# K and V in 4 MB loads over four slots instead of 2 MB loads over eight, with PV of the second half moved behind all its scores

## The chip, the core, the metric

One core of one Trainium2 chip runs one program. The metric is device time in microseconds (us). A ratio is the mean time of one kernel's runs over the mean time of the other's runs of the same rounds, so it is not quite the ratio of the medians that are quoted beside it.

## The reference, cut to what matters

The program is one decode step of a transformer block: two sequences, one new token each, and a cache of 32,768 keys and values for each of 4 key/value heads. Each key/value head serves 8 query heads. A small modulation and query projection come first; an output projection and a two-layer MLP come last.

```python
B, Sq, D = (2, 1, 1024)
Hq, Hkv, Sk, Dh = (32, 4, 32768, 128)
...
scores = jnp.einsum('bhqd,bhkd->bhqk', q, k) * Dh ** (-0.5)
p = _softmax(scores, axis=-1)
o = jnp.einsum('bhqk,bhkd->bhqd', p, v)
```

K and V together are 2 x 2 x 4 x 32,768 x 128 bf16 values, 134 MB. All the weights are another 44 MB. Every byte is used once. So the question for this kernel is how well its loads keep the DMA engines busy.

## The kernel before

There are 8 rounds, one for each pair of sequence and key/value head. In a round, K comes in 4 chunks of 8,192 rows. PE transposes a chunk in 8 groups, VectorE and ScalarE copy the result out of PSUM, and PE multiplies it with the 8 queries. Softmax and PV (probabilities times V) of a round run one round later, between the chunks of the next K. One chunk of K or V is one load of 2 MB, and each kind and chunk has its own 16 KB slot (per partition).

```python
SLOT = {("K", 0): 0, ("K", 1): 1, ("V", 0): 2, ("V", 1): 3, ("K", 2): 4, ("V", 2): 5, ("K", 3): 6, ("V", 3): 7}
...
add((kind, i, cc), [TPC, D], cache[b, g][r0:r0 + CH_ROWS, :].rearrange("(p t) d -> p t d", p=128),
    SLOT[kind, cc] * 16 * KB, f"{kind}{cc}")
...
order = [("K", 0), ("K", 1), ("V", 0), ("V", 1), ("K", 2), ("V", 2), ("K", 3), ("V", 3)]
early = [("V", 0), ("V", 1), ("K", 0), ("K", 1), ("K", 2), ("V", 2), ("K", 3), ("V", 3)]
```

All loads form one list. SyncE issues them strictly in that order. Before each issue it waits until the last reader of the slot's old content is done. So one load that must wait for its slot holds back everything behind it.

```python
for cc in range(NCH):
    for g8 in range(TPC // 8):
        tr(i, cc, g8)                 # transposes: the last reader of a K slot
        ...
    if cc == 1:
        lagged(lambda: pv(i - 1, 0), row_sums, lambda: pv(i - 1, 1))
    elif cc > 1:
        lagged(lambda: pv(i - 1, cc)) # the last reader of a V slot
```

## Time and profile before

| | before |
|---|---|
| median of 3 runs | 423.7 us (423.6 to 423.91) |
| span of the profiled run | 421.8 us |
| bytes moved, mean rate | 178.47 MB, 423 GB/s |
| share of the load queue's packets in 16 engines' span | 99.1% |
| PE, VectorE, ScalarE busy | 71%, 40%, 37% |
| last landing to the end of the span | 415.98 to 421.8 us |

These lines are from the page of the kernel before. The rows PEclk, DMA and GB/s are the span in 40 equal slices: granted PE clock and busy share of the DMA engines in tenths, and the rate. The group line ends with PE's idle time just before such instructions and what ended it. The last two lines give count, size and median time from issue to landing of the loads.

```profile
span 421.8 us, 11638 instructions
...
PEclk9999999969989999796988997898899696655565
DMA  8999999999999999999999999999999999999995
GB/s 334 429 431 423 435 432 423 429 432 426 433 432 429 435 429 430 435 429 429 435 429 432 437 423 433 435 426 433 433 428 433 430 430 435 427 429 424 428 423 244
DMA packets 14335, 178.47 MB, mean 423 GB/s; under 512 B 1513, under 2 KB 1520, under 8 KB 2802
q1 hardware_dynamic: 14322, 178.29, 99.1%
...
DMA 80%; PE 16%; ACT 2%; SPq 1%; issue 0%; DVE 0%
...
L542 PE MATMUL psKT<-ident,K 128*128 128x128 bf16 x2048 | 173.8, 237 | 39.0 <-DMA K<-in_A_k_cache_dram 37.8
...
K<-in_A_k_cache_dram SPq DMA_DIRECT2D x32, 2048.0 KB, 31.6
V<-in_A_v_cache_dram SPq DMA_DIRECT2D x32, 2048.0 KB, 35.1
```

No slice between the first and the last is under 423 GB/s, and PE is the one that waits. The Trainium skill ("DMA: Bandwidth & Descriptors", section Where 436 GB/s comes from) puts the ceiling of a core's 16 DMA engines at 435 GB/s. This trace agrees: 431 GB/s over 120 to 340 us. Only two things can shorten this kernel: a cheaper stream of bytes, or a shorter start or end.

Tools are used below, all of them made from the trace's records of single DMA packets and of the issues.

- *Packet time*: how long the record of a packet lasts. In the load queue a 4-byte packet, which each engine writes at the end of a load, takes 9 ns; 8,192 B take 309.5 ns; 16,384 B take 611 ns.
- *Outstanding*: the bytes of all loads issued before a moment, less the bytes of the packets finished by then.
- *Loss* of a stretch: its length less its bytes at 430 GB/s.

Here is what the packet records say of the kernel before (counted over the load queue; size in bytes, number, ns of one; 305 packets of other sizes are left out):

```
      4   1473     9.0
   7168   1024   272.0
   8192   1792   309.5
  12288   1024   469.3
  16384   8704   611.5
```

The 8,704 packets of 16,384 B are the K and V loads (64 x 128) and the wo loads (4 x 128). So "16 KB per packet" is not new in the change: a partition's 64 rows of a chunk lie together in memory, and the kernel before already moved them as one packet.

### The profile page before, as it was taken

The numbers are of one execution on the slowest core, as the hardware profiler recorded it, in microseconds if no ns is written. First come the engines' busy times: TensorE is split into PE (matmuls) and PEld (weight loads), VectorE is DVE, ScalarE is ACT, GpSimd is POOL, SyncE is SP. The second block draws the span as 40 slices with busy tenths as digits, with TensorE's granted clock in tenths as the row PEclk, the third lists the DMA queues.
The fourth block names the chain that finished last, engine by engine and source line by source line (L and its number), as shares of the span: only waits on it lengthen the run. The fifth ranks groups of instructions, "written<-read, shape, count | busy, mean of one in ns | idle before, by whom it ended". The sixth has DMA issues, their size and how long they took to land.

```text
span 421.8 us, 11638 instructions
## 1 busy us (share of the span) xinstructions
PE 299.5 (71%) x5171; PEld 238.1 (56%) x5171; DVE 167.1 (40%) x347; ACT 156.6 (37%) x269; POOL 6.0 (1%) x31
## 2 busy tenths in 40 slices
PE   1547478878997688587877848796888682445576
PEld 1105158866975678476767828684776671112244
DVE  1102026644663476155534724652474352101311
ACT  2000025547645349142833633383447245000020
POOL 3000000000000000000000000000000000000000
PEclk9999999969989999796988997898899696655565
DMA  8999999999999999999999999999999999999995
GB/s 334 429 431 423 435 432 423 429 432 426 433 432 429 435 429 430 435 429 429 435 429 432 437 423 433 435 426 433 433 428 433 430 430 435 427 429 424 428 423 244
DMA packets 14335, 178.47 MB, mean 423 GB/s; under 512 B 1513, under 2 KB 1520, under 8 KB 2802
## 3 DMA queue, kind: packets, MB, share of 16 engines
q1 hardware_dynamic: 14322, 178.29, 99.1%
q8 instruction: 9, 0.15, 0.1%
q14 instruction: 4, 0.03, 0.0%
HBM read 178.28 MB, written 0.00 MB: 423 GB/s over the span
## 4 chain that ended last, share of the span: by engine, by line
DMA 80%; PE 16%; ACT 2%; SPq 1%; issue 0%; DVE 0%
DMA K<-in_A_k_cache_dram 60%; PE psKT L542 11%; DMA wo<-in_A_wo_dram 8%; DMA w<-in_B_w_dram 7%; DMA wmod<-in_w_mod_dram 4%; PE psS L554 3%; ACT E_sb L575 1%; PE psO L584 1%; SPq L415 1%; ACT KT_sb L546 1%; PE psO L757 1%; PE psS L678 0%; ACT L575 0%; PE psM L565 0%; ACT S_sb L558 0%
## 5 line engine op out<-in xcount | busy, mean ns | idle before, releaser
L542 PE MATMUL psKT<-ident,K 128*128 128x128 bf16 x2048 | 173.8, 237 | 39.0 <-DMA K<-in_A_k_cache_dram 37.8
L542 PEld LDWEIGHTS psKT<-ident,K 128*128 128x128 bf16 x2048 | 133.2, 106 | 49.7 <-DMA K<-in_A_k_cache_dram 44.9
L548 DVE COPY KT_sb<-psKT 128x1024 bf16<-128x1024 bf16 x160 | 108.3, 689 | 112.5 <-PE psKT L542 112.5
L546 ACT ACTIVATE KT_sb<-psKT 128x1024 bf16<-128x1024 bf16 x96 | 98.0, 1020 | 131.2 <-PE psKT L542 131.2
L554 PE MATMUL psS<-qcur,KT_sb 128*128 128x8 bf16 x2048 | 88.2, 167 | 8.1 <-ACT KT_sb L546 6.7
L554 PEld LDWEIGHTS psS<-qcur,KT_sb 128*128 128x128 bf16 x2048 | 79.5, 99 | 13.2 <-ACT KT_sb L546 8.1
L584 PE MATMUL psO<-V,E_sb 128*32 128x512 bf16 x512 | 35.5, 403 | 6.3 <-DMA V<-in_A_v_cache_dram 5.0
L575 ACT ACTIVATE E_sb<-S_sb,negm 128x256 bf16<-128x256 f32 x64 | 32.3, 504 | 7.7 <-DVE negm L571 6.8
L559 DVE TENSOR_REDUCE m1c<-psS 128x8 f32<-128x512 f32 x32 | 22.1, 691 | 14.4 <-ACT S_sb L558 13.3
L558 ACT ACTIVATE S_sb<-psS 128x512 f32<-128x512 f32 x32 | 19.0, 592 | 14.1 <-PE psS L554 14.1
L584 PEld LDWEIGHTS psO<-V,E_sb 128*32 128x32 bf16 x512 | 11.5, 100 | 16.8 <-DMA V<-in_A_v_cache_dram 5.7
L491 PE MATMUL psS<-wmod,inT 128*32 128x512 bf16 x64 | 8.4, 622 | 11.9 <-DMA wmod<-in_w_mod_dram 11.9
L678 PE MATMUL psS<-wo,atT 128*32 128x512 bf16 x64 | 7.6, 627 | 11.3 <-DMA wo<-in_A_wo_dram 11.3
L462 ACT ACTIVATE stat<-stat 128x2 f32<-128x2 f32 x3 | 0.6, 204 | 38.9 <-DVE stat L461 38.9
L512 PE MATMUL psS<-wq,inT 128*32 128x512 bf16 x64 | 7.6, 627 | 6.9 <-DMA wq<-in_A_wq_dram 5.9
L575 ACT ACTIVATION_READ_ACCUMULATOR E_sb<-S_sb,negm 128x1 f32 x64 | 12.1, 189 | 0.0
L491 PEld LDWEIGHTS psS<-wmod,inT 128*32 128x32 bf16 x64 | 1.3, 112 | 17.9 <-DMA wmod<-in_w_mod_dram 17.4
L678 PEld LDWEIGHTS psS<-wo,atT 128*32 128x32 bf16 x64 | 1.9, 128 | 16.3 <-DMA wo<-in_A_wo_dram 10.3
L604 PE MATMUL psM<-msum,hmat 128*128 128x128 f32 x16 | 4.4, 359 | 7.1 <-DVE msum L599 7.1
L497 ACT ACTIVATE S_sb<-psS 128x512 f32<-128x512 f32 x1 | 0.6, 597 | 22.8 <-DVE S_sb L499 22.8
L499 DVE COPY S_sb<-psS 128x512 f32<-128x512 f32 x1 | 0.7, 692 | 20.6 <-PE psS L491 20.6
L599 DVE SCALAR_TENSOR_TENSOR msum<-psO,mk,msum 128x128 f32<-128x128 f32 x24 | 8.4, 351 | 0.8
(116 smaller groups left out, 132.3 us busy)
## 6 DMA issues: line engine op xcount, KB each, us to landing
K<-in_A_k_cache_dram SPq DMA_DIRECT2D x32, 2048.0 KB, 31.6
V<-in_A_v_cache_dram SPq DMA_DIRECT2D x32, 2048.0 KB, 35.1
wmod<-in_w_mod_dram SPq DMA_DIRECT2D x8, 1536.0 KB, 16.5
wq<-in_A_wq_dram SPq DMA_DIRECT2D x4, 2048.0 KB, 37.5
wo<-in_A_wo_dram SPq DMA_DIRECT2D x4, 2048.0 KB, 29.0
w<-in_B_w_dram SPq DMA_DIRECT2D x4, 1792.0 KB, 39.1
w<-in_B_w_dram SPq DMA_DIRECT2D x3, 2048.0 KB, 30.6
w<-in_B_w_dram SPq DMA_DIRECT2D x1, 768.0 KB, 28.0
```

Of the source, the lines that this page charges most:

```text
L491: pe(lambda e, w=it.view, k=k, ch=ch, n=n, q=q: e.matmul(bank[n][32 * q:32 * q + 32, :], lhsT=inT[:, k, :], rhs=w[:, ch * 512:(ch + 1) * 512],
L512: pe(lambda e, w=it.view, k=k, ch=ch, n=n, q=q: e.matmul(bank[n][32 * q:32 * q + 32, :], lhsT=inT[:, k, :], rhs=w[:, k % 2, ch * 512:(ch + ...
L542: pe(lambda e, kq=kq, jj=jj, w=it.view, t=t: e.transpose(psKT[kq][:, jj * 128:(jj + 1) * 128], w[:, t, :], ident[:, :]), reads=[it.reg, "i ...
L546: act(lambda e, src=src: e.activation(KT_sb[g8][:, :, :], src, ACT.Copy), reads=[f"psKT{kq}"], writes=[f"KT_sb{g8}"], sem=f"ev{cc}_{g8}")
L548: dve(lambda e, src=src: e.tensor_copy(KT_sb[g8][:, :, :], src), reads=[f"psKT{kq}"], writes=[f"KT_sb{g8}"], sem=f"ev{cc}_{g8}")
L554: pe(lambda e, t=t, jj=jj: e.matmul(ps[:, t * HPG:(t + 1) * HPG], lhsT=KT_sb[g8][:, jj, :], rhs=qcur[:, :], start=True, stop=True), reads= ...
L558: act(lambda e: e.activation(Sc, ps[:, :].rearrange("p (t h) -> p h t", h=HPG), ACT.Copy), reads=[preg], writes=[f"S_sb{i % 2}_{cc}"], sem ...
L559: dve(lambda e: e.tensor_reduce(m1c[:, :, cc], ps[:, :].rearrange("p (t h) -> p h t", h=HPG), AX.X, ALU.max), reads=[preg], writes=[f"m1c{ ...
L575: act(lambda e: e.activation(E_sb[:, :, h, :], S_sb[j][:, h, :].rearrange("p (u t) -> p u t", t=4), ACT.Exp, bias=negm[:, h:h + 1], scale= ...
L584: pe(lambda e, t4=t4, tg=tg, q=q: e.matmul(psO[32 * q:32 * q + 32, :], lhsT=E_sb[:, tg // 4, :, :].rearrange("p h t -> p (h t)"), rhs=it.v ...
L599: dve(lambda e, q=q: e.scalar_tensor_tensor(out=msum[:, :], in0=psO[:, q * 128:(q + 1) * 128], scalar=mk4[:, q:q + 1], in1=msum[:, :], op0 ...
L678: pe(lambda e, w=it.view, g=g, j=j, hf=hf, q=q: e.matmul(psS[0][32 * q:32 * q + 32, :], lhsT=atT[g][:, j, :], rhs=w[:, j, hf * 512:(hf + 1 ...
```

## The change

Two chunks become one load of 4 MB, which takes one of four 32 KB slots. A slot now comes free only when both of its chunks have been read. PV of chunk 2 moves behind the scores of chunk 3, so that PE does not wait for the second V load in the middle of the second half of K. The number of issues halves and the bytes stay.

```diff
-    SLOT = {("K", 0): 0, ("K", 1): 1, ("V", 0): 2, ("V", 1): 3, ("K", 2): 4, ("V", 2): 5, ("K", 3): 6, ("V", 3): 7}
+    SLOT = {("K", 0): 0, ("V", 0): 1, ("K", 1): 2, ("V", 1): 3}
...
-        add((kind, i, cc), [TPC, D], cache[b, g][r0:r0 + CH_ROWS, :].rearrange("(p t) d -> p t d", p=128),
-            SLOT[kind, cc] * 16 * KB, f"{kind}{cc}")
+        add((kind, i, hf), [2, TPC * D], cache[b, g][r0:r0 + 2 * CH_ROWS, :].rearrange("(c p t) d -> p c (t d)", c=2, p=128),
+            SLOT[kind, hf] * 32 * KB, f"{kind}{hf}")
...
-    order = [("K", 0), ("K", 1), ("V", 0), ("V", 1), ("K", 2), ("V", 2), ("K", 3), ("V", 3)]
-    early = [("V", 0), ("V", 1), ("K", 0), ("K", 1), ("K", 2), ("V", 2), ("K", 3), ("V", 3)]
+    order = [("K", 0), ("V", 0), ("K", 1), ("V", 1)]
+    early = [("V", 0), ("K", 0), ("K", 1), ("V", 1)]
...
-            elif cc > 1:
-                lagged(lambda: pv(i - 1, cc))
+            elif cc == 3:
+                lagged(lambda: pv(i - 1, 2), lambda: pv(i - 1, 3))
```

What is cut: the same split of an index into half and chunk in the transposes and in PV, and new offsets for one w1 load and one w2 load.

More of the change, by code (lines that the diff above doesn't have):

```diff
@@ L368, in add, with add_kv @@
         by_key[key] = it
-    SLOT = {("K", 0): 0, ("K", 1): 1, ("V", 0): 2, ("V", 1): 3, ("K", 2): 4, ("V", 2): 5, ("K", 3): 6, ("V", 3): 7}
-    def add_kv(kind, i, cc):
+    SLOT = {("K", 0): 0, ("V", 0): 1, ("K", 1): 2, ("V", 1): 3}
+    def add_kv(kind, i, hf):
         cache = A_k_cache if kind == "K" else A_v_cache
         b, g = i % 2, i // 2
-        r0 = cc * CH_ROWS
-        add((kind, i, cc), [TPC, D], cache[b, g][r0:r0 + CH_ROWS, :].rearrange("(p t) d -> p t d", p=128),
-            SLOT[kind, cc] * 16 * KB, f"{kind}{cc}")
+        r0 = hf * 2 * CH_ROWS
+        add((kind, i, hf), [2, TPC * D], cache[b, g][r0:r0 + 2 * CH_ROWS, :].rearrange("(c p t) d -> p c (t d)", c=2, p=128),
+            SLOT[kind, hf] * 32 * KB, f"{kind}{hf}")
     wm_v = w_mod.rearrange("(p k) n -> p k n", k=KT8)
@@ L383, in bass_adaLN_cond__gqa_block_cached__mixer_channel_mlp__decode_kernel @@
         add(("wq", k), [2, HQ * D], A_wq[k * 256:(k + 1) * 256, :].rearrange("(k p) n -> p k n", p=128), (96 + 16 * k) * KB)
-    for cc in range(4):
-        add_kv("K", 0, cc)
-    order = [("K", 0), ("K", 1), ("V", 0), ("V", 1), ("K", 2), ("V", 2), ("K", 3), ("V", 3)]
-    early = [("V", 0), ("V", 1), ("K", 0), ("K", 1), ("K", 2), ("V", 2), ("K", 3), ("V", 3)]
+    add_kv("K", 0, 0)
+    add_kv("K", 0, 1)
+    order = [("K", 0), ("V", 0), ("K", 1), ("V", 1)]
+    early = [("V", 0), ("K", 0), ("K", 1), ("V", 1)]
     for i in range(1, NBG + 1):
-        for kind, cc in early if i == 1 else order:
+        for kind, hf in early if i == 1 else order:
             if kind == "V":
-                add_kv("V", i - 1, cc)
+                add_kv("V", i - 1, hf)
             elif i < NBG:
-                add_kv("K", i, cc)
+                add_kv("K", i, hf)
     for g, off in enumerate((128, 144, 0, 16)):
         add(("wo", g), [8, DM], A_wo[g * 1024:(g + 1) * 1024, :].rearrange("(p j) n -> p j n", j=8), off * KB)
-    for k, off in enumerate((64, 96, 32, 48)):
+    for k, off in enumerate((64, 80, 32, 48)):
         add(("w1", k), [2, F], B_w1[k * 256:(k + 1) * 256, :].rearrange("(k p) n -> p k n", p=128), off * KB)
     w2_v = B_w2.rearrange("(q p j) n -> p q (j n)", p=128, j=4)
-    for k, off in enumerate((80, 112, 128)):
+    for k, off in enumerate((96, 112, 128)):
         add(("w2", k), [2, 4 * DM], w2_v[:, 2 * k:2 * k + 2, :], off * KB)
@@ L537, in tr @@
     def tr(i, cc, g8):
-        it = need("K", i, cc)
+        it = need("K", i, cc // 2)
+        kt = it.view[:, cc % 2, :].rearrange("p (t d) -> p t d", d=D)
         kq = g8 % NPKT
@@ L541, in tr @@
             t = g8 * 8 + jj
-            pe(lambda e, kq=kq, jj=jj, w=it.view, t=t: e.transpose(psKT[kq][:, jj * 128:(jj + 1) * 128], w[:, t, :], ident[:, :]),
+            pe(lambda e, kq=kq, jj=jj, w=kt, t=t: e.transpose(psKT[kq][:, jj * 128:(jj + 1) * 128], w[:, t, :], ident[:, :]),
                reads=[it.reg, "ident"], writes=[f"psKT{kq}"], mark=(jj == 7))
@@ L579, in pv @@
     def pv(i, cc):
-        it = need("V", i, cc)
+        it = need("V", i, cc // 2)
+        vt = it.view[:, cc % 2, :]
         for t4 in range(TPC // 4):
@@ L584, in pv @@
             pe(lambda e, t4=t4, tg=tg, q=q: e.matmul(psO[32 * q:32 * q + 32, :], lhsT=E_sb[:, tg // 4, :, :].rearrange("p h t -> p (h t)"),
-                                                    rhs=it.view[:, t4 * 4:t4 * 4 + 4, :].rearrange("p t d -> p (t d)"),
+                                                    rhs=vt[:, t4 * 512:(t4 + 1) * 512],
                                                     start=(cc == 0 and t4 < 4), stop=(cc == NCH - 1 and t4 >= TPC // 4 - 4),
```

## The prediction

> **What bounds the kernel now.** The DMA engines, nearly from first byte to last. The page of before: 178.3 MB in 421.8 us, 423 GB/s, the queue's packets taking 99.1% of the 16 engines' span; between the first and last slice 422 to 437 GB/s. The Trainium skill ("DMA: Bandwidth & Descriptors", section Where 436 GB/s comes from) gives a ceiling of 435 GB/s; this trace agrees, with 430 to 433 in the windows of the K/V stage. PE is busy 71%, DVE 40%, ACT 37%; PE waits for K (37.8 us in the groups); the chain of waits gives DMA 80%. Not DMA time: the start (first slice 334 GB/s) and the 5.8 us after the last landing (415.98).
>
> **What the change touches.**
> - Packet size: nothing. The trace's packet records already hold 8,704 packets of 16,384 B (K, V and wo), 611 ns each.
> - Loads: 64 become 32. Each ends with a 4-byte packet per engine of 9 ns; 32 fewer save about 0.3 us (estimate). Setup and landing latency are hidden: at every K/V issue at least 5.2 MB is outstanding (bytes issued less bytes landed). SyncE's 0.33 us per issue is off the path.
> - Slots: same 128 KB, half as many, so one comes free only after two chunks. This is the danger: the queue could run dry. Estimates from before's landing times and PE times (a chunk takes 6.6 us after idling, 5.2 us warm, PV of a chunk 1 us; the first round with exponentials takes 13.8 us for two chunks):
>  - first K reload: slot free near 74, queue fed until 81;
>  - second: near 84.5, fed until 91;
>  - K of the third round: near 105, fed until 110.6;
>  - steady rounds (39 us of DMA, 27 of PE): 15 us left;
>  - last V load, which waits for the deferred PV: near 348.3, fed until 354.
>  The thinnest margin is 5 to 6 us, over 2 MB; before it was about 12 us.[...]
> - PE: bursts and pauses twice as long, so maybe more work at the lower granted clock; PE has a third of its time to spare.
> - Deferred PV: it delays one V slot (counted above). After the last V landing two chunks of PV remain instead of one, 1 us, hidden behind the wo, w1 and w2 loads queued by then.
>
> **Critical path.** Only the 0.3 us of end packets lies on it.
>
> **Predicted time.** 423.4 us (423.7 less 0.3), range 422.4 to 424.9. Faster by over 2%: 1%; within 2%: 96%; slower by over 2%: 3%.
>
> **What would show the steps.** DMA slices 9 throughout with 425 to 435 GB/s; about 13,800 packets (512 fewer); K and V issues 16 each of 4,096 KB, still 20 to 35 us to landing; PE's wait for K about as long in total, in fewer and longer waits; mean granted clock equal or a little lower. If the queue ran dry, a slice between 75 and 115 us, or near 350 us, would fall below 400 GB/s, and the span would grow by that hole.
>
> **What would make it wrong.** (1) A dry spell at a thin margin: a few us. (2) Alternating between two runs 2 MB apart slows the reads: packets would take over 611 ns; the wq loads, two runs 1 MB apart, ran at 427 GB/s, so I doubt it. (3) SyncE stalls while issuing (wq, two packets per partition, blocked it 3 to 7 us when much was outstanding), harmless while the queue is full.

## The result, and the profile after

| | before | after |
|---|---|---|
| median | 423.73 us (423.6 to 423.91, 6 runs) | 423.51 us (423.41 to 424.64, 6 runs) |
| ratio after / before | | 1.0001, interval 0.9988 to 1.0014 |
| span of the profiled run | 421.8 us | 422.8 us (the 424.64 us run) |

The time is the same. But the runs of after are not one heap: four lie at 423.41 to 423.58, just under before, and two at 424.21 and 424.64. The profiled run is the slowest of them. These are the lines of its page that answer to those above.

```profile
span 422.8 us, 11591 instructions
...
PEclk9999757989999698988788896969887888665566
DMA  8999999999999999999999999999999999999995
GB/s 334 430 429 424 437 426 432 427 398 429 432 428 434 429 429 434 429 432 432 429 434 429 432 434 427 436 428 432 434 428 436 428 432 434 428 432 420 428 425 227
DMA packets 13822, 178.46 MB, mean 422 GB/s; under 512 B 1001, under 2 KB 1008, under 8 KB 2290
q1 hardware_dynamic: 13810, 178.28, 99.0%
...
DMA 70%; PE 26%; ACT 2%; SPq 1%; issue 0%; DVE 0%
...
L543 PE MATMUL psKT<-ident,K 128*128 128x128 bf16 x2048 | 178.0, 240 | 43.3 <-DMA K<-in_A_k_cache_dram 41.9
...
K<-in_A_k_cache_dram SPq DMA_DIRECT2D x16, 4096.0 KB, 25.8
V<-in_A_v_cache_dram SPq DMA_DIRECT2D x16, 4096.0 KB, 32.6
```

Almost every line says what it said before. There are 512 packets under 512 B fewer, which is 32 loads x 16 engines. PE waits for K about as long in total. One thing stands out: the ninth slice (84.6 to 95.1 us) moved 398 GB/s. It also shows what does not mean much here. The chain gives DMA 70% instead of 80%, though the kernel is as DMA-bound as before, because the chain only changes over to PE where a reload waited for PE to free its slot.

The same place, from the windows of the same run (columns: stretch, its us, busy us of each engine with instruction counts, granted clock, DMA share, GB/s) and from the timeline of SyncE:

```profile
85.00:90.00 5.00, 4.03 (x102) 3.82 (x99) 3.27 (x5) 3.09 (x4) 0.00 (x0) 1.00 1.03 436
90.00:95.00 5.00, 3.21 (x48) 2.50 (x45) 2.07 (x5) 1.62 (x2) 0.19 (x1) 0.79 0.96 367
```

```profile
88.51 0.37 SPq L415 DMA_DIRECT2D K<-in_A_k_cache_dram  x1
```

That issue is the second K reload of the kernel (round 1, second half). It had to wait until PE had transposed chunk 3 of round 0. When it went out, 1.15 MB was outstanding, 2.7 us of work at 430 GB/s. The packet records show what followed: between 85 and 97 us, 38 of the 294 packets of 16,384 B took over 640 ns, up to 1,411 ns, and from 90 to 94 us the stream moved 317, 317, 388 and 393 GB/s, us by us. In these 4 us the rate was 18% under 430 GB/s, but the DMA engines' busy share fell only from 1.01 to 0.95, so most of this hole is packets that took longer, and the lesser part is engines with nothing to do. Why those packets took longer is not shown. The loss between 85 and 120 us is 0.85 us; in the kernel before it is 0.02 us. (Another 0.4 us of this run's excess over the 423.39 us run shown below is lost in its last 8 us, and nothing here explains that.)

Why was the slot freed so late? PE's timeline between 74.5 and 90 us shows three pauses that wait for nothing the profile knows (in brackets: the idle time before the group and its cause).

```profile
76.88 0.62 PE L543 MATMUL psKT<-ident,K 128*128 128x128 bf16 x8 [1.42 <-issue]
83.18 0.30 PE L555 MATMUL psS<-qcur,KT_sb 128*128 128x8 bf16 x6 [1.13 <-issue]
89.36 0.80 PE L555 MATMUL psS<-qcur,KT_sb 128*128 128x8 bf16 x16 [0.88 <-issue]
```

Only the first two, 2.55 us together, can have delayed the slot: the third begins at 88.48 us, when the transposes of chunk 3 are done.

The packet records have a second queue, named "instruction", with packets of 16,384 B at 74.51, 80.68 and 87.12 us, each 0.89 to 0.95 us long. That they are the instructions PE paused for is an inference from the times; no run here tests it. The fit is loose: these packets had ended when the pauses began (0.0 to 0.5 us before), and the one at 67.21 us has no such pause beside it. There are five of them between 67 and 93 us, in the first two rounds, and then none until 369 us, which fits a loop whose body is fetched once.

### The profile page after: what moved, and what is told of

Its sections match the earlier page's. It is cut to its first block, busy times and chain, and to the rows that moved or that the text cites. A ratio compares the mean times of both kernels' runs of the same rounds, so it can differ in the third digit from the quotient of the medians.

```text
span 422.8 us, 11591 instructions
## 1 busy us (share of the span) xinstructions
PE 299.2 (71%) x5171; PEld 241.2 (57%) x5171; DVE 167.3 (40%) x347; ACT 156.2 (37%) x269; POOL 6.0 (1%) x31
## 4 chain that ended last, share of the span: by engine, by line
DMA 70%; PE 26%; ACT 2%; SPq 1%; issue 0%; DVE 0%
DMA K<-in_A_k_cache_dram 50%; PE psKT L543 18%; DMA wo<-in_A_wo_dram 8%; DMA w<-in_B_w_dram 7%; PE psS L555 5%; DMA wmod<-in_w_mod_dram 4%; ACT E_sb L576 1%; SPq L415 1%; PE psO L586 1%; ACT KT_sb L547 1%; PE psO L759 1%; ACT L576 0%; PE psS L680 0%; PE psM L566 0%; ACT S_sb L559 0%
## 5 line engine op out<-in xcount | busy, mean ns | idle before, releaser
L543 PE MATMUL psKT<-ident,K 128*128 128x128 bf16 x2048 | 178.0, 240 | 43.3 <-DMA K<-in_A_k_cache_dram 41.9
L543 PEld LDWEIGHTS psKT<-ident,K 128*128 128x128 bf16 x2048 | 137.0, 108 | 51.0 <-DMA K<-in_A_k_cache_dram 46.0
L555 PE MATMUL psS<-qcur,KT_sb 128*128 128x8 bf16 x2048 | 88.6, 168 | 8.2 <-ACT KT_sb L547 6.1
L586 PE MATMUL psO<-V,E_sb 128*32 128x512 bf16 x512 | 33.8, 399 | 1.4 <-ACT E_sb L576 1.3
L680 PE MATMUL psS<-wo,atT 128*32 128x512 bf16 x64 | 6.7, 566 | 12.5 <-DMA wo<-in_A_wo_dram 12.5
L599 DVE TENSOR_SCALAR msum<-psO,mk 128x128 f32<-128x128 f32 x8 | 2.8, 351 | 15.1 <-PE psO L586 15.1
```

The lines of the kernel that those rows point to most:

```text
L543: pe(lambda e, kq=kq, jj=jj, w=kt, t=t: e.transpose(psKT[kq][:, jj * 128:(jj + 1) * 128], w[:, t, :], ident[:, :]), reads=[it.reg, "ident" ...
L555: pe(lambda e, t=t, jj=jj: e.matmul(ps[:, t * HPG:(t + 1) * HPG], lhsT=KT_sb[g8][:, jj, :], rhs=qcur[:, :], start=True, stop=True), reads= ...
L586: pe(lambda e, t4=t4, tg=tg, q=q: e.matmul(psO[32 * q:32 * q + 32, :], lhsT=E_sb[:, tg // 4, :, :].rearrange("p h t -> p (h t)"), rhs=vt[: ...
L680: pe(lambda e, w=it.view, g=g, j=j, hf=hf, q=q: e.matmul(psS[0][32 * q:32 * q + 32, :], lhsT=atT[g][:, j, :], rhs=w[:, j, hf * 512:(hf + 1 ...
```

## The experiments

The theory to test: the DMA stream sets the time. A load that is queued costs almost nothing by itself, so half as many loads gain almost nothing, and the slots' layout matters only where the queue runs low. The rival: larger loads (or the deferral) were a real gain, and the coarser slots gave it back. All kernels here computed the right result.

### The order of loads in the first round with V

```diff
-    early = [("V", 0), ("K", 0), ("K", 1), ("V", 1)]
+    early = [("V", 0), ("K", 0), ("V", 1), ("K", 1)]
```

The slot of the second V half is free since the weights in it were read. Put ahead of the second K reload, its 4 MB bridge the wait.

> The changed kernel, but in the first round with V the second V load stands before the second K reload instead of after it. Theory (queue ran low): in the changed kernel's profile the second K reload is issued at 88.5 us with 1.15 MB outstanding, packets behind it take up to 1.4 us instead of 0.611, and about 0.8 us is lost between 90 and 95 us; with the V load ahead, over 5 MB is outstanding at that reload, no slice between 75 and 115 us is under 420 GB/s, and all runs lie at 423.3 to 423.6 us. Rival (the runs of 424.2 and 424.6 us were chance, not the low queue): the spread stays, some runs again over 424.

Measured: 423.36 us (423.27 to 423.6, 5 runs) beside 423.55 us of before; ratio 0.9995 (0.9982 to 1.0008). The second K reload now goes out at 87.47 us with 5.75 MB outstanding. The windows show the hole gone (416 GB/s follows 436 in the window before; over 85 to 120 us the loss is 0.08 us):

```profile
85.00:90.00 5.00, 3.53 (x90) 3.22 (x86) 2.58 (x4) 2.52 (x4) 0.19 (x1) 1.00 1.03 436
90.00:95.00 5.00, 2.76 (x23) 2.15 (x24) 1.85 (x4) 0.96 (x2) 0.00 (x0) 0.70 0.98 416
```

To see whether this was luck, the changed kernel and this form ran once more, on one chip.

> The changed kernel again, unedited, beside the early-V form on the same chip. Theory (its spread comes from how much is outstanding at the second K reload): runs between 423.3 and 424.7 us, spread over 0.5 us, the profiled run slower than the early-V one by about what it loses between 85 and 120 us. Rival (the first spread was chance): spread under 0.3 us, no difference from the early-V form.

> The early-V form again (the second V load ahead of the second K reload in the first round with V). Theory: all runs within 0.4 us, near 423.3 to 423.6, mean 0.1 to 0.6 us under the unedited changed kernel's mean on this chip. Rival: same spread and mean as that.

Measured: the changed kernel 423.53 us (423.39 to 425.76, 6 runs); the early-V form 423.45 us (423.39 to 423.58, 5 runs); before 423.64 us. The expectation that the profiled run of the changed kernel would be the slower one missed, and that miss is the best evidence. (The 425.76 us run also lies above the range expected.) This time the profile fell on a run of 423.39 us, and the hole was not there:

```profile
85.00:90.00 5.00, 3.51 (x89) 3.21 (x86) 2.71 (x5) 2.62 (x4) 0.19 (x1) 1.00 1.02 433
90.00:95.00 5.00, 2.64 (x22) 2.03 (x23) 1.63 (x4) 0.72 (x1) 0.00 (x0) 0.72 1.00 423
```

```profile
87.45 0.37 SPq L415 DMA_DIRECT2D K<-in_A_k_cache_dram  x1
```

So the same program, 1.06 us earlier at this one issue, lost nothing. The 1.06 us are PE's: the first K reload went out 0.25 us earlier (75.06 us), and the two pauses before the second took 1.18 and 0.55 us instead of 1.42 and 1.13:

```profile
76.39 0.62 PE L543 MATMUL psKT<-ident,K 128*128 128x128 bf16 x8 [1.18 <-issue]
82.12 0.30 PE L555 MATMUL psS<-qcur,KT_sb 128*128 128x8 bf16 x6 [0.55 <-issue]
```

| profiled run | second K reload issued at | outstanding | loss 85 to 120 us | its time |
|---|---|---|---|---|
| changed kernel, first | 88.51 us | 1.15 MB | 0.85 us | 424.64 us |
| changed kernel, again | 87.45 us | 1.62 MB | 0.08 us | 423.39 us |
| early V | 87.47 us | 5.75 MB | 0.08 us | 423.37 us |
| early V, again | 87.01 us | 5.96 MB | 0.09 us | 423.58 us |

Over both sets, 3 of the 12 runs of the changed kernel are over 424 us (424.21, 424.64, 425.76), and none of the 10 runs of the early-V form. By chance alone that would come about once in seven times, so the count by itself proves little. The pair with 32 KB packets below repeats the test: 3 of 6 runs without the early V load are over 1 us slower than the fastest of their form, and none of 5 with it (the two pairs together: about once in sixty). It also parts lateness from depth: its profiled runs issue the second K reload at 88.46 us with 1.24 MB outstanding (loss 0.61 us) and at 88.59 us, no earlier, with 5.41 MB (no loss). Only the runs that were profiled show their hole, so for the 424.21 and 425.76 us runs the cause is likely and not shown.

### The deferral alone, and the loads alone

The kernel before with only the deferral:

```diff
-            elif cc > 1:
-                lagged(lambda: pv(i - 1, cc))
+            elif cc == 3:
+                lagged(lambda: pv(i - 1, 2), lambda: pv(i - 1, 3))
```

> The kernel before (2 MB loads, eight slots) with only the other half of the change: PV of chunks 2 and 3 after all scores. Theory (PE order is off the path while the queue is fed): 423.7 us, ratio 1.000 within 0.001; the outstanding bytes at the last V issues fall a little. Rival (the deferral itself gains or costs something that the loads hide): over 0.3% away.

Measured: 423.69 us (4 runs) beside 423.70 us, ratio 1.0001. As expected, the deferral does nothing by itself. The smallest amount outstanding at a V issue fell from 5.24 to 3.16 MB and cost nothing.

The changed kernel with that edit turned round (PV of chunk 2 again between the chunks):

> The changed kernel without the deferral: PV of chunk 2 again stands between the chunks of the second half, so PE must wait for the whole second V load there. Theory (PE has slack): PE's waits for V grow to roughly 3 to 5 us in a round, K's second slot is freed some 5 us later, still 10 us before the queue is empty; time as the changed kernel, 423.4 to 424.6 us. Rival (the deferral is needed with 4 MB loads): the later frees drain the queue, 2 us or more slower.

Measured: 426.62 us (425.04 to 427.47, 4 runs) beside 423.70 us, ratio 1.0057 (1.0038 to 1.0077). The theory's number missed: with 4 MB loads the deferral is needed. But the reason is not the steady rounds. There PE waits for V 15.0 us in 5 waits between 120 and 345 us, as expected, and K's second slot is freed later, yet 4.0 MB or more stayed outstanding at every reload from 119 to 320 us, and the window from 120 to 340 us moves 432 GB/s, as much as the early-V form. The loss is at two places:

```profile
90.00:95.00 5.00, 3.54 (x47) 2.75 (x44) 2.37 (x5) 1.42 (x2) 0.19 (x1) 0.50 0.91 341
350.00:355.00 5.00, 4.60 (x116) 3.84 (x112) 3.79 (x8) 2.73 (x4) 0.00 (x0) 1.00 0.83 354
355.00:360.00 5.00, 1.31 (x6) 0.74 (x6) 2.54 (x9) 1.31 (x5) 0.22 (x1) 0.84 0.97 344
```

The first is the hole already known (issue at 89.82 us, 0.54 MB outstanding, loss 1.18 us). The second is new. PE's timeline shows how it arises: in the last round of the loop, PE stands 3.02 us in the middle of the second half for V, and the PV that frees the last V slot ends at 353.9 us.

```profile
346.63 1.05 PE L586 MATMUL psO<-V,E_sb 128*32 128x512 bf16 x16 [3.02 <-DMA V<-in_A_v_cache_dram]
352.87 1.05 PE L586 MATMUL psO<-V,E_sb 128*32 128x512 bf16 x16
```

In the changed kernel both PVs run in one go after the scores:

```profile
349.00 1.91 PE L586 MATMUL psO<-V,E_sb 128*32 128x512 bf16 x32
```

So the last V load goes out at 350.96 us with 1.55 MB outstanding there (loss between 340 and 372 us: none), but at 353.96 us with 0.34 MB without the deferral (loss 1.81 us). No run moves that load alone, so this cause is read from the traces. To tell the two holes apart, the early-V order was added to the form without deferral:

> No deferral, but the early-V order, so that only the last V load is short. In the run without deferral that load was issued at 354.0 us with 0.34 MB outstanding and 1.8 us were lost between 340 and 372 us; 1.2 us were lost between 85 and 120 us. Theory: the first loss is gone and the second stays: about 425.3 us, that is 1.6 to 2.2 us over the early-V form. Rival (what the deferral avoids is PE's waits in the steady rounds, not the last V load): the time stays near 426.6 us.

Measured: 426.44 us (425.97 to 427.37, 4 runs) beside 423.64 us, ratio 1.0072. By its time this is the rival's number. By its profile (the run of 426.12 us) the rival fails: the loss from 85 to 120 us is down to 0.09 us, the steady rounds again move 432 GB/s, and at the last V load the hole is there, 0.14 MB outstanding and 2.15 us lost:

```profile
90.00:95.00 5.00, 2.64 (x22) 2.03 (x23) 1.76 (x4) 1.23 (x2) 0.14 (x1) 0.50 1.00 426
350.00:355.00 5.00, 4.35 (x109) 3.60 (x105) 3.76 (x9) 2.63 (x4) 0.00 (x0) 1.00 0.81 311
355.00:360.00 5.00, 1.67 (x6) 0.90 (x6) 2.31 (x8) 0.97 (x3) 0.22 (x1) 0.59 0.91 367
```

The span is 2.7 us over the early-V form's (424.3 against 421.6), of which 2.15 us are in that hole. Why removing the first hole did not lower the mean is open: four runs, spread over 1.4 us, with the depth of the second hole differing between the two profiles (1.81 and 2.15 us).

### What a load costs, and what a packet costs

The kernel before with two 8 KB packets per partition in each 2 MB load:

```diff
-        add((kind, i, cc), [TPC, D], cache[b, g][r0:r0 + CH_ROWS, :].rearrange("(p t) d -> p t d", p=128),
+        add((kind, i, cc), [2, TPC // 2 * D], cache[b, g][r0:r0 + CH_ROWS, :].rearrange("(c p t) d -> p c (t d)", c=2, p=128),
```

(Cut: the same split in the transposes and in PV.)

> The kernel before (2 MB loads, eight slots), but each load has two packets of 8 KB per partition. Theory (8 ns per packet on each engine): 512 more packets per engine, 4.1 us more: 427.8 us, DMA slices near 426 GB/s. Rival (bytes alone bind): 423.7 us.

Measured: 426.06 us (4 runs) beside 423.55 us, ratio 1.0058. Between the two numbers expected: smaller packets do cost, 2.46 us (means 426.06 and 423.60) for 512 more per engine, so 4.8 ns each. The packet records say 8 ns each (2 x 309.5 less 611). The records of an engine overlap a little (the DMA share of a stretch reads up to 1.03), which may hide the rest. A packet here is one consecutive stretch of memory, so no run tells the number of packets from the length of the stretches read.

The same with each load issued as two loads of 1 MB:

```diff
+                halves = [lambda e, d=cur.view, s=cur.src, c=c: e.dma_start(d[:, c, :], s[:, c, :]) for c in range(2)]
+                T.dma("sp", halves, key=cur.sem, writes=[cur.reg], frees=old)
```

(The slot's semaphore counts 32 for a load pair instead of 16.)

> The 8 KB-packet form of the kernel before, with each 2 MB load issued as two loads of 1 MB; packets unchanged, 64 more loads. Theory (a queued load costs the stream only its end packet, 9 ns per engine): 0.6 us over the 8 KB form with 2 MB loads, so about 428.4 us. Rival (a load's setup and landing are partly exposed, so that halving the loads was a real gain which the changed kernel gave back elsewhere): 64 more loads at even 0.1 us are 6 us, so 434 us or more[...].

Measured: 426.41 us (4 runs), against 426.06 us of the form with 2 MB loads; the ratios to before are 1.0063 and 1.0058. By the means (426.39 and 426.06), 64 more loads cost 0.33 us, 5 ns each. The two forms ran on different chips, whose kernels before differ by 0.07 us in the mean, and against its own kernel before each form lies 2.46 and 2.72 us higher, 0.26 us apart or 4 ns a load. The intervals of the two ratios (1.0044 to 1.0073, 1.0047 to 1.008) overlap, so 5 ns is a rough figure; the rival's 6 us or more is out of reach. This settles the main question. The Trainium skill ("DMA: Bandwidth & Descriptors", section Anatomy of one DMA) fits one DMA issued from GpSimd with 2.0 us plus its bytes, and it puts most of the 2 us down to the confirmation that the last byte has landed. The loads here are issued by SyncE, and no run shows one on its own, so that figure is not tested. In this queue, which always has more loads behind (4.6 MB or more at every K and V issue from 65 us on), the cost seen is some 5 ns a load, near the 9 ns record of its end packet.

The changed kernel with 128 consecutive rows per partition, so one packet of 32 KB instead of two of 16 KB (K and V are permuted alike, so softmax and PV give the same):

```diff
-        add((kind, i, hf), [2, TPC * D], cache[b, g][r0:r0 + 2 * CH_ROWS, :].rearrange("(c p t) d -> p c (t d)", c=2, p=128),
+        add((kind, i, hf), [2 * TPC * D], cache[b, g][r0:r0 + 2 * CH_ROWS, :].rearrange("(p t) d -> p (t d)", p=128),
```

(Cut: the same change of view in the transposes and in PV.)

> The changed kernel, but a partition takes 128 consecutive rows, so each load has one packet of 32 KB per partition instead of two of 16 KB. Theory (each packet costs bytes/27.2 GB/s plus about 8 ns, from 16,384 B in 611 ns and 8,192 B in 309.5 ns): packets of about 1,214 ns, 256 fewer per engine, 2.0 us less: 421.4 us, up to 422.6 in runs where the queue runs low at the second K reload. Rival (bytes alone bind at this packet size): 423.4 us, packets of 1,222 ns, or they are cut to 16 KB again.

Measured: 422.78 us (422.13 to 424.3, 6 runs) beside 423.55 us, ratio 0.998 (0.9967 to 0.9992). The packets are 32,768 B long and take 1,213 ns. The spread of over 2 us goes with the low queue, but is explained only in part: the profiled run (424.3 us) issued its second K reload at 88.46 us with 1.24 MB outstanding and lost 0.61 us between 85 and 120 us, while its span is 2.0 us over that of the form below (422.4 against 420.4). The rest lies in smaller losses later, half of them in the last 8 us, whose cause is not shown. Both edits together:

> Both edits: 32 KB packets and the second V load ahead of the second K reload in the first round with V. Theory: 421.4 us (2.3 us, 0.55%, under the kernel before), all runs within 0.3 us. Rivals as for the two edits alone: 423.4 us, or a spread of over 0.8 us.

Measured: 422.19 us (422.01 to 422.37, 5 runs) beside 423.55 us, ratio 0.9967 (0.9954 to 0.998). This is the fastest kernel, 0.33% under the one before. Its windows move 433 GB/s between 120 and 340 us, against 431 before. Against the early-V form (means 422.21 and 423.39) the larger packets gain 1.18 us for 256 fewer per engine: 4.6 ns a packet, the same as from the other side. The expected 2.0 us was too large because it took the record's 8 ns. From its page:

```profile
span 420.4 us, 11591 instructions
...
DMA packets 9726, 178.46 MB, mean 425 GB/s; under 512 B 1001, under 2 KB 1008, under 8 KB 2290
```

### Fewer slots

The changed kernel with both V halves in one slot, 12 MB of slots instead of 16:

```diff
-    SLOT = {("K", 0): 0, ("V", 0): 1, ("K", 1): 2, ("V", 1): 3}
+    SLOT = {("K", 0): 0, ("V", 0): 1, ("K", 1): 2, ("V", 1): 1}
```

(The V loads then share one semaphore, which counts 32 a round.)

> The changed kernel with both V halves in one 32 KB slot: 12 MB of slots instead of 16. Theory (time is lost only where the queue is empty, and where is told by adding landing times and PE times): no loss in the steady rounds (estimated queue left at a reload 7 us), an empty queue of about 8 us near 101 to 110 us (the second V load waits for the first PV), about 6 us near 344 to 350, about 4 us near 360 to 364: 15 to 20 us slower, about 440 us. Rival (the depth of the queue itself matters everywhere): DMA slices under 420 GB/s in the steady rounds too, and more than 25 us slower.

Measured: 452.95 and 455.66 us beside 423.70 us, ratio 1.0723 (1.0686 to 1.076). The expectation missed by half: about 30 us are lost, not 15 to 20. By its numbers (over 25 us, slices under 420 GB/s in the steady rounds) the rival is met. The rows of the slices show where (the span is 451.1 us, so a slice is 11.3 us):

```profile
DMA  8999999993999999999989999999999855999995
GB/s 342 430 426 426 437 430 431 420 384 121 427 434 433 415 434 426 399 431 429 436 366 430 430 409 421 427 434 379 433 430 411 342 215 212 430 427 423 427 427 237
```

Yet most of the loss is in three empty stretches, at the three loads expected, the last two of them some 15 us later for the time lost before: 9.6 us lost between 85 and 120 us, 14.2 us between 340 and 414 us (expected 8 and 10). What was not expected are the slices of 366 to 415 GB/s between them, 5 us in all (loss from 120 to 340 us: 4.6 us, against a small gain of 0.7 us in the changed kernel by the same measure). The V reloads of the steady rounds went out with 0.13 to 2.7 MB outstanding, not with the estimated 7 us (3 MB). My estimate of PE's time in a half was again too short. Two of these places, summed us by us: after an issue at 266.5 us with 1.13 MB outstanding 0.8 us were lost, after one at 306.7 us with 0.95 MB 1.2 us. So the depth does not matter everywhere, but a low queue costs before it is quite empty.

The kept traces tell how low. Take every K and V issue after 60 us in the nine profiled runs with 4 MB loads, and the loss of the 10 us that follow. All 15 issues with 1.24 MB or less outstanding (under 2.9 us of work) lost 0.35 to 1.86 us. All 33 with 1.47 to 3.1 MB lost 0.16 us at most. Only at the second K reload did an experiment set the depth (the early V load); the other places are observed, and nothing lies between 1.24 and 1.47 MB, so this is an observation about this stream and no rule.

## Why the prediction was right

The predicted 423.4 us, "same" at 96%, was met by 423.51 us. Step by step:

- *The DMA stream sets the time; loads cost only their end packets* (0.3 us saved): right, and the size is of that order. A queued load costs some 5 ns, so 32 fewer save 0.17 us; the early-V form, which has the fewer loads and no hole, is 0.2 us under before on both chips (means 423.39 and 423.60; 423.47 and 423.66). Both are inside the interval of the ratio (0.9982 to 1.0008), so neither is clear of noise.
- *Packet size does not change*: right, 8,704 packets of 16,384 B before and after, at 611 ns. So the doubt that two runs 2 MB apart might slow the reads is answered too.
- *The queue stays fed, thinnest margin 5 to 6 us*: this step was too hopeful. First K reload: predicted at 74 us, measured 75.31. Third round: 105, measured 105.92. Steady rounds: 15 us left, measured 5.6 MB or more at every K reload from 135 to 310 us, 13 us or more. But the second K reload was put at 84.5 us and came at 88.51, and the last V load was put at 348.3 us and came at 350.96. Of the 4.0 us at the second K reload, 1.3 us were there at the first, and 2.7 us came in the two chunks between. The term at fault for these is the time of a chunk, "5.2 us warm". The trace of before already held the right one: its K reloads of the first round are issued at 65.08, 70.26, 76.66 and 83.55 us, so its third and fourth chunks took 6.4 and 6.9 us, with PE's pauses in them. Two such chunks from 75.3 us give 88.6. What made the last V load 2.7 us late is not worked out.
- *The thinnest margin is enough*: it held in most runs and not in all. With 2.7 us left 0.85 us were lost, with 3.8 us left nothing. The prediction set the margin against the delay until first bytes move. That delay is 1.02 to 1.03 us where the queue was empty (v_one_slot, issues at 108.24, 365.13 and 380.67 us), so it alone does not explain a loss with 2.7 us left: the slower packets above do, for a reason that stays open. The signal that the prediction named for it, a slice under 400 GB/s between 75 and 115 us, is there: 398.
- *The deferred PV only delays a V slot*: half right. Against the kernel before it costs nothing. But it is not idle in the change: without it the last V load comes 3 us later, and the kernel is 0.57% slower than before. The prediction never asked what the deferral was for.
- *PE's share*: PE's wait for K 41.9 us instead of 37.8, clock 0.832 instead of 0.855 in the profiled runs. No effect on the time shows, as said: the three fastest runs of after had 0.795 to 0.808.

So the median came out right on its own (0.2 us gained, 0.3 us said), and the mean is no different from before's because two small terms nearly cancel: about 0.2 us gained in every run, and 0.7 to 2.3 us lost in perhaps a quarter of them (3 of 12). That the thin margin cost no more in most runs was luck as much as foresight: it was half of what the prediction took it for.

## What to carry to other kernels

When the DMA engines are busy from end to end, ask what a change does to the stream itself: fewer and larger packets paid (4.7 ns each), fewer loads hardly did (5 ns each, and there are far fewer of them). Before making slots coarser, write down for every reload when its slot comes free and how many bytes are still outstanding then, with durations from that very stretch of the trace, above all in the first round and at the last load, where the order of loads can often be changed for nothing. If some runs of a kernel are slower than the rest, look for the place where its queue is lowest.

## What the Trainium skill lacked or had wrong

- "DMA: Bandwidth & Descriptors", section Anatomy of one DMA: the 2.0 us per DMA is fitted for DMAs issued from GpSimd; what a load issued by SyncE costs in a queue that stays fed is not told. Here it is about 5 ns (0.33 us for 64 loads).
- The same page, section Bandwidth (Why small descriptors are slow), knows a small fixed cost per packet, but calls joining descriptors into packets only worth it at 256 B or less, and the page "Perfetto Trace Analysis", section DMA Optimizations, speaks of overhead under 2 KB. Neither gives a figure for far larger packets, where the runs (which lengthen the consecutive stretches, and join nothing) show a further gain: 8 to 16 KB 2.46 us, 16 to 32 KB 1.18 us of 424 us, some 4.7 ns a packet on each engine.
- No page says how much must be outstanding when a load is issued. Here 1.15 MB at one place lost 0.85 us and 1.62 MB there lost nothing, and over nine traces all 15 issues at 1.24 MB or less lost time while all 33 at 1.47 to 3.1 MB lost at most 0.16 us; after a low point packets of 16,384 B took up to 1.4 us instead of 0.611.
- The page "Runtime: NRT & Kernel Launch", section Instruction fetch mechanics, has the refilling of instructions, but no duration of such a packet beside a busy load stream. The records show packets of 16,384 B and about 0.9 us each, and PE pauses of 0.9 to 1.4 us that follow three of them in the first rounds; that the two belong together is not tested.
